# K of the second attention in rows of 8192 B, two tiles a load, with another table of rankings

## The chip, the cores and the metric

The kernel runs on one core of a Trainium2 chip. The metric is the device time of one execution in microseconds; the runs below give it as a median. TensorE (PE) multiplies matrices into PSUM, VectorE (DVE) and ScalarE (ACT) work on SBUF and PSUM, SyncE (SP) issues nearly all transfers from HBM, GpSimd (POOL) sets up constants and issues seven of the output transfers. 16 DMA engines move the data.

## What is computed

Two independent attention blocks, A and B, with cached K and V, and their outputs side by side. A shares one K/V head among eight query heads; B has a K/V head for each of its 32 query heads.

```python
# both: B=16, Sq=32, D=1024, 32 query heads, Sk=1024, Dh=128; all bf16
# A: k_cache, v_cache are (16, 4, 1024, 128); B: (16, 32, 1024, 128)
def _B_ref(x, k_cache, v_cache, wq, wo):
    q = (x @ wq).reshape(B, Sq, H, Dh).transpose(0, 2, 1, 3)
    scores = jnp.einsum("bhqd,bhkd->bhqk", q, k_cache) * (Dh ** -0.5)
    p = _softmax(scores, axis=-1)
    o = jnp.einsum("bhqk,bhkd->bhqd", p, v_cache)
    return o.transpose(0, 2, 1, 3).reshape(B, Sq, H * Dh) @ wo
# A is the same with K and V repeated eight times over the heads
return jnp.concatenate([a, b], axis=-1)
```

K and V of B are 134.2 MB each, K and V of A 16.8 MB each, the four weights 8.4 MB each.

## The kernel before

**Steps.** The work is a list of operations (`pr.add`), built in 128 steps. A step handles one quad of A (four heads of one batch entry, 128 query rows); every second step handles a pair of B: two quads, that is four heads for two batch entries. A pair of B uses four tiles of K and four of V, numbered x = 4 n to 4 n + 3 for pair n. A tile is 512 KB: two heads of one batch entry, 128 partitions by 4096 B.

**K of B.** `tile_src` (L901 to L904) lays two neighbouring heads over the 128 partitions, 16 rows of K (4096 B) on each partition. `st_dmaKB` (L906 to L913) issues the load of one tile on SP. Its place comes from `home_k`: one of eight slots of `KB_sb`, or, for some of the last tiles, a quarter of `wq_sb`, which is no longer needed then. `st_ktrB` (L976) transposes each tile in place on VectorE in blocks of 32 by 32, taking two bf16 as one f32. After this a partition holds a pair of head dimensions, and the free dimension runs over the 16 rows held by a partition and, within these, over 32 source partitions. `st_scoresB` then computes the scores in four passes (`fp`), each a matmul of 512 K columns for each of four tiles x, two quads and two partition groups; the operands are 32 by 32, and 16 matmuls can run beside one another on the sixteen small tiles of the array. L1027 is the line of these matmuls. The bf16 columns are picked with a step of 2, as two head dimensions are interleaved:

```python
rhs = tile_k(4 * q.pn + x)[r0:r0 + 32, :].rearrange("p (s x) -> p s x", s=16)[:, :, o0:o0 + 63:2]
```

**After the scores.** `st_max` (L1038, VectorE) reduces a quad's scores to the negative maximum, `st_exp` (L1051, ScalarE) exponentiates from PSUM into `P2_sb`, and its access pattern puts the columns into the order in which V lies. TensorE then transposes the probabilities (L1097; L1063 is the same for A), they are copied out of PSUM (L651), and L1116 multiplies them with V. L1174 and L1175 normalise; L1190 and L1182 transpose the result for the output projection (L823), whose sums are kept in `acc` (L835, L844). The query projections are L735 (A) and L754 (B); L995 is the score matmul of A, L1083 its product with V, L969 the transposition of its K, L671 that of x at the start.

**Buffers.** There are eight slots for K of B (two pairs), six for V (one and a half), two each for K and V of A. A load is issued on SP when the last reader of the slot's former content has finished; SP takes its instructions in order, so a load that waits holds up those behind it. L891, L898, L910 and L955 are the issues for K of A, V of A, K of B and V of B, L714 those of the query weights, L795 and L805 those of the output weights.

**Order.** `list_schedule` simulates the engines and the transfers with durations written in tables (`DUR` for instructions, `PACKET` for the time of one DMA row by its size) and picks, at each turn, one ready operation by rank. `RANKS` holds 16 ways of ranking, and `TUNE` names for each window of 77 operations which of them applies. The result is the fixed order of each engine, with PSUM banks and work buffers assigned; semaphores are then set for what crosses engines.

Of the kernel before, what the change touches and what calls it, by code (L numbers as in the profile page):

```python
# [43 lines left out]
RANKS = ((3.5, 122, 0.35, 0.0, 0.3), (3.0, 122, 0.35, 0.0, 0.3), (4.0, 122, 0.35, 0.0, 0.3), (3.5, 122, 0.15, 0.0, 0.3), (2.5, 122, 0.35, 0.0, 0.3), (5.0, 122, 0.35, 0.0, 0.3),  # L44
         (3.5, 122, 0.7, 0.0, 0.3), (3.5, 120, 0.35, 0.0, 0.3), (3.0, 124, 0.2, 0.0, 0.3), (3.5, 122, 0.15, 1.5, 0.3), (3.5, 122, 0.15, -1.5, 0.3), (3.5, 122, 0.15, 0.0, 0.0),
         (3.5, 122, 0.15, 0.0, 0.7), (3.5, 122, 0.15, 4.0, 0.3), (3.5, 122, 0.15, -4.0, 0.3), (3.5, 122, 0.25, 0.0, 0.3))
TUNE = (6, 7, 1, 5, 6, 8, 8, 8, 8, 8, 8, 11, 5, 15, 1, 9, 0, 1, 5, 1, 7, 14,
        15, 12, 12, 10, 12, 12, 15, 3, 12, 14, 7, 13, 13, 13, 13, 13, 7, 6, 10, 1, 12, 10,
        3, 12, 0, 11, 9, 12, 7, 13, 12, 11, 12, 3, 4, 10, 14, 9, 9, 10, 4, 0, 0)
HOLD_AHEAD = 1  # L50
STEP_NEAR = 0
TAIL_BASE = 12.0
# [17 lines left out]
    "c0": (0.2, 0.1), "c1": (0.3, 0.1),  # L70
}

PACKET = {"kb_dma": (4096, 0.1592), "vb_dma": (4096, 0.1592), "outh_dma": (1024, 0.049), "wqh_dma": (1024, 0.049)}
PACKET_DEFAULT = (2048, 0.0847)
DMA_ISSUE = 0.45
DMA_FIRST = 1.4
# [3 lines left out]
def dma_time(op):  # L80
    size, us = PACKET.get(op.name, PACKET_DEFAULT)
    return op.dur / size * us / 16
# [45 lines left out]
class Prog:  # L128
# [120 lines left out]
    def list_schedule(self, lat=0.05, look=LOOK):  # L249
# [170 lines left out]
        while True:  # L420
            best = None
            bkey = None
            turn = len(order) // WINDOW
            turn = TUNE[turn] if turn < len(TUNE) else 0
            bl, look, act_first = ranks[turn], RANKS[turn][2], RANKS[turn][4]
# [127 lines left out]
def build(nc, pa, pb, out):  # L553
# [6 lines left out]
    Dh = pa["k"].shape[3]  # L560
    Sk = pa["k"].shape[2]
# [6 lines left out]
    MS = 4  # L568
# [9 lines left out]
    NIT = NSB * NG * 8  # L578
# [7 lines left out]
    pr = Prog()  # L586
    stack = contextlib.ExitStack()
    with stack:
        def sb(name, shape, dt):
            return stack.enter_context(nc.sbuf_tensor(name, shape, dt))  # L590
# [8 lines left out]
        wq_sb = sb("wq_sb", [P, DJ, 2 * CW], BF)  # L599
# [9 lines left out]
        KB_sb = sb("KB_sb", [P, NKB, 16 * Dh], BF)  # L609
# [14 lines left out]
        def bank(v):  # L624
            return psum[:, v.idx, :]
# [7 lines left out]
        for idt, key in ((ident, "ident"), (id32, "id32")):  # L633
            pr.add("pool", lambda g, idt=idt: g.memset(idt[:], 0.0), writes=[key], name="c0")
            pr.add("pool", lambda g, idt=idt: g.affine_select(idt[:], idt[:], [[1, P]], ALU.not_equal, 1.0, base=0, channel_multiplier=-1),
                   writes=[key], name="c1")
# [233 lines left out]
        def mk_quadB(t):  # L870
            q = Quad()
            q.pi = 1
            q.t = t
            q.m = t // (NG * 4)
            q.G = (t // 4) % NG
            jb = t % 4
            q.bp = jb // 2
            q.e = jb % 2
            q.pn = t // 2
            q.b0 = 4 * q.G + 2 * q.bp  # L880
            q.first_of_group = (jb == 0)
            q.last_of_group = (jb == 3)
            q.qid = ("B", t)
            q.kid = ("B", t)
            return q
# [15 lines left out]
        def tile_src(key, x):  # L901
            q, i = quadsB[2 * (x // 4)], x % 4
            h = q.m * MS + 2 * (i % 2)
            return pb[key][q.b0 + i // 2, h:h + 2].rearrange("e (p s) d -> (e p) (s d)", s=16)  # L904

        def st_dmaKB(x):  # L906
            if x < 2 * NIT:
                kind, sl = home_k(x)
                pr.step, was = 2 * ((x - NKB) // 4) if x >= NKB else pr.step, pr.step
                pr.add("sp", lambda e: e.dma_start(tile_k(x), tile_src("k", x)), writes=[(kind, sl)], dma_key=f"{kind.lower()}{sl}", name="kb_dma",  # L910
                       dur=2 * Sk * Dh * 2, wtag={(kind, sl): x})
                pr.step = was

        V_LAST = 2 * NIT - 4
# [12 lines left out]
        def kb_of(x):  # L927
            r = (x - XK) % (NKB + 4)
            assert r >= 4
            return (XK + r - 4) % NKB  # L930

        def home_k(x):
            if x < XK:
                return ("KB", x % NKB)
            return ("wq", (x - XK) % (NKB + 4)) if (x - XK) % (NKB + 4) < 4 else ("KB", kb_of(x))

        def tile_k(x):
            kind, sl = home_k(x)
            return wq_sb[:, 2 * sl:2 * sl + 2, :].rearrange("p j c -> p (j c)") if kind == "wq" else KB_sb[:, sl, :]
# [39 lines left out]
        def both(vS):  # L979
            return psum[:, vS[0].idx:vS[0].idx + 2, :]  # L980

        def score_buf(q):
            q.vS = [Virt("bank", "S"), Virt("bank", "S")]
            q.vst, q.vbo = Virt("stat"), Virt("bank")
# [15 lines left out]
        def p2_of(v):  # L1000
            return P2_sb[:, v.idx, :] if isinstance(v, Virt) else xT_sb[:, v[1], :, :].rearrange("p j t -> p (j t)")[:, 0:2 * Sk]
# [7 lines left out]
        def st_scoresB(qs):  # L1009
            n = qs[0].pn  # L1010
            vP, vPT = (("xT", 0, 0), (("xT", 0, 1), ("xT", 0, 2))) if n >= XT_FREE and n % 2 else (Virt("P2"), (Virt("PT2"), Virt("PT2")))
            for q in qs:
                score_buf(q)
                q.vP, q.vPT, q.vO = vP, vPT, Virt("O2")
            q0 = qs[0]
            gp = (q0.m * NG + q0.G) % 2

            def e_s(e, fp):
                last = None
                o0 = (fp // 2) * 64 + fp % 2  # L1020
                for x in range(4):
                    for q in qs:
                        for g2 in range(2):
                            r0 = 32 * (2 * q.e + g2)
                            lhsT = QR[r0:r0 + 32, gp, 2 * q.bp + x // 2, x % 2, o0:o0 + 63:2]
                            rhs = tile_k(4 * q.pn + x)[r0:r0 + 32, :].rearrange("p (s x) -> p s x", s=16)[:, :, o0:o0 + 63:2]
                            last = e.matmul(bank(q.vS[g2])[32 * x:32 * x + 32, :].rearrange("p (s j) -> p s j", s=16), lhsT, rhs,  # L1027
                                            start=(fp == 0), stop=(fp == 3), tile_position=(r0, 32 * x))
                return last
            qr = [("QR", gp, 2 * q0.bp + t_) for t_ in range(2)]  # L1030
            kt = [(home_k(4 * q0.pn + x), ("T", 4 * q0.pn + x)) for x in range(4)]
            for fp_ in range(4):
                pr.add("pe", lambda e, fp_=fp_: e_s(e, fp_), reads=qr + [r_ for r_, _ in kt], writes=[r_ for q in qs for r_ in q.vS],
                       name="scoresB", tag="B%d" % q0.t, rtag=dict([(r_, (q0.m, q0.G)) for r_ in qr] + kt))
# [6 lines left out]
        def st_exp(q):  # L1041
            vS, vP, vst = q.vS, q.vP, q.vst

            def emit(e):
                if q.pi == 0:
                    src = both(vS).rearrange("p u (c k) -> p k u c", c=NCH // 2)
                    dst = P_sb[:, vP.idx, :].rearrange("p (k u c) -> p k u c", u=2, c=NCH // 2)
                else:
                    src = both(vS).rearrange("p g (s j) -> p g j s", s=16)
                    dst = p2_of(vP)[:, q.e * Sk:(q.e + 1) * Sk].rearrange("p (g j s) -> p g j s", g=2, s=16)  # L1050
                return e.activation(dst, src, ACTF.Exp, bias=stat[:, vst.idx, 0:1], scale=1.0, accum_out=stat[:, vst.idx, 1:2])  # L1051
            pr.add("act", emit, writes=vS + [vP, vst], name="exp")

# [146 lines left out]
        quadsB = [mk_quadB(t) for t in range(NIT)]  # L1200
# [8 lines left out]
        def pairB(n):  # L1209
            qs = [quadsB[2 * n], quadsB[2 * n + 1]]  # L1210
            for x in range(4):
                st_ktrB(4 * n + x)
            if n == 0:
                for x in range(4, NKB):
                    st_dmaKB(x)
            st_scoresB(qs)
            while k_next[0] < min(2 * NIT, 4 * n + 4 + NKB + (4 if n >= LATE else 0)):
                st_dmaKB(k_next[0])
                k_next[0] += 1
            if 4 * n == V_LAST - 8:  # L1220
                for x in (0, 2, 1, 3):
                    st_dmaVB(V_LAST + x)
            for q in qs:
                st_max(q)
                st_exp(q)
            st_ptB(qs)
            if 4 * n == V_LAST:
                st_last(qs)
                return
            st_pvB(qs)  # L1230
            while v_next[0] < min(V_LAST, 4 * n + 4 + NVB + (4 if n >= LATE else 0)):
                st_dmaVB(v_next[0])
                v_next[0] += 1
            for q in qs:
                st_recip(q)
                st_norm(q)
                st_otr(q)
# [30 lines left out]
        for x in range(4):  # L1268
            st_dmaKB(x)
# [90 lines left out]
        if SCHED:  # L1360
            pr = pr.list_schedule()
# [10 lines left out]
def bass_concat_heads__gqa_block_cached__mha_block_cached__near_ridge_kernel(nc, A_x, A_k_cache, A_v_cache, A_wq, A_wo, B_x, B_k_cache, B_v_cache, B_wq, B_wo, out):  # L1372
    build(nc, dict(x=A_x, k=A_k_cache, v=A_v_cache, wq=A_wq, wo=A_wo),
          dict(x=B_x, k=B_k_cache, v=B_v_cache, wq=B_wq, wo=B_wo), out)
# [28 lines left out]
```

## Time and profile before

| | |
|---|---|
| median of three runs | 850.98 us (850.81 to 852.41) |
| span of the profiled execution | 849.5 us |
| PE, DVE, ACT busy | 783.0, 727.0, 623.6 us |
| moved | 341.68 MB, mean 402 GB/s |

The profile is of one execution, and its span runs from its first to its last instruction; the runs' time is taken from outside, so it holds about 1.5 us more. "Busy" of PE counts stretches in which any matmul is under way, and ends of matmuls are modelled. A group's line gives busy time, the mean of one instruction in ns, and the idle time just before its instructions with what ended it. PEld is the weight load, which overlaps the matmuls. SPq is SP's DMA queue. Rates in GB/s are those of all 16 DMA engines.

### The profile page before, as it was taken

What the parts mean: (1) busy time and instruction counts of PE and PEld (TensorE: products, weight loads), DVE (VectorE), ACT (ScalarE), POOL (GpSimd) and SP (SyncE); (2) the same over time, 40 slices, a digit from 0 to 9 for tenths busy, and PEclk for the clock granted to TensorE, in tenths of its full rate; (3) what the DMA queues carried; (4) which work ended last, traced back from release to release, by engine and by line L of the source; (5) the groups of instructions that cost most, each with busy time, mean ns of one, the idle gap of its engine ahead of it and who ended that gap; (6) DMA issues with size and microseconds to landing.
All of it is one profiled execution on the core that took longest, in us unless ns stands there. A gap on an engine that the chain in (4) does not pass through costs nothing.

```text
span 849.5 us, 29749 instructions
## 1 busy us (share of the span) xinstructions
PE 783.0 (92%) x13056; PEld 522.6 (62%) x13056; DVE 727.0 (86%) x1018; ACT 623.6 (73%) x1363; POOL 6.1 (1%) x20
## 2 busy tenths in 40 slices
PE   7989999999898999998999988999899998899878
PEld 4456665666565566665666665666666666666655
DVE  1499987979799898987999898998999978998995
ACT  3497787778677777786788787677877867686874
POOL 1000000000000000000000000000000000000000
PEclk9999999999999999999999999999999999999999
DMA  9999999999999999999999999999999999999995
GB/s 339 415 412 414 411 411 410 405 393 394 416 384 412 409 395 415 416 398 412 414 392 408 411 392 416 415 416 405 410 402 415 412 414 415 415 400 414 416 418 226
DMA packets 112208, 341.68 MB, mean 402 GB/s; under 512 B 12048, under 2 KB 12304, under 8 KB 112080
## 3 DMA queue, kind: packets, MB, share of 16 engines
q1 hardware_dynamic: 111520, 337.95, 100.0%
q8 instruction: 103, 1.69, 0.7%
q0 software_dynamic: 560, 1.84, 0.5%
q14 instruction: 25, 0.20, 0.1%
HBM read 337.64 MB, written 2.10 MB: 400 GB/s over the span
## 4 chain that ended last, share of the span: by engine, by line
PE 55%; DVE 23%; ACT 14%; DMA 5%; issue 2%; SPq 1%; DVEq 0%; ACTq 0%
DVE stat L1038 10%; PE psum L1116 10%; PE psum L823 10%; DVE KB_sb L976 8%; ACT P_sb L1051 8%; PE psum L1027 6%; PE psum L1063 5%; PE psum L754 5%; PE psum L1097 5%; PE psum L1083 4%; DMA KB_sb<-in_B_k_cache_dram 4%; PE psum L995 4%; PE psum L735 4%; ACT PT_sb L651 2%; ACT O_sb L1174 1%
## 5 line engine op out<-in xcount | busy, mean ns | idle before, releaser
L1038 DVE TENSOR_REDUCE stat<-psum 128x1 f32<-128x1024 f32 x256 | 303.6, 1210 | 50.7 <-PE psum L995 31.5
L1051 ACT ACTIVATE P_sb<-psum,stat 128x1024 bf16<-128x1024 f32 x246 | 275.9, 1122 | 63.2 <-DVE stat L1038 59.7
L976 DVE STREAM_TRANSPOSE KB_sb<-KB_sb 128x1024 f32<-128x1024 f32 x240 | 286.6, 1222 | 6.2 <-DMA KB_sb<-in_B_k_cache_dram 6.0
L651 ACT COPY PT_sb<-psum 128x512 f32<-128x512 f32 x226 | 131.4, 604 | 35.2 <-PE psum L1063 22.0
L1116 PE MATMUL psum<-VB_sb,PT_sb 64*64 64x256 bf16 x3584 | 116.2, 271 | 8.6 <-ACT P_sb L1051 5.2
L1116 PEld LDWEIGHTS psum<-VB_sb,PT_sb 64*64 64x64 bf16 x3584 | 97.0, 107 | 27.7 <-issue 25.5
L1174 ACT ACTIVATE O_sb<-psum,stat 128x128 bf16<-128x128 f32 (+1 forms) x205 | 80.8, 417 | 43.2 <-PE psum L1083 23.1
L1063 PE MATMUL psum<-id,P_sb 128*128 128x128 f32 x512 | 88.7, 297 | 6.9 <-ACT P_sb L1051 4.1
L1063 PEld LDWEIGHTS psum<-id,P_sb 128*128 128x128 f32 x512 | 74.0, 208 | 25.2 <-ACT P_sb L1051 13.8
L995 PE MATMUL psum<-KTA_sb,QT_sb 128*128 128x512 bf16 x256 | 84.4, 384 | 3.1 <-ACT P_sb L1051 1.6
L1083 PE MATMUL psum<-VA_sb,PT_sb 128*128 128x128 bf16 x1024 | 78.8, 221 | 7.5 <-ACT P_sb L1051 2.6
L1083 PEld LDWEIGHTS psum<-VA_sb,PT_sb 128*128 128x128 bf16 x1024 | 63.2, 99 | 31.6 <-issue 12.0
L1027 PE MATMUL psum<-KB_sb,QR 32*32 32x512 bf16 x3840 | 73.3, 394 | 8.1 <-ACT P_sb L1051 4.6
L1097 PE MATMUL psum<-id,P_sb 128*128 128x128 f32 x472 | 76.2, 287 | 4.1 <-ACT P_sb L1051 3.5
L754 PE MATMUL psum<-wq_sb,xT_sb 128*128 128x512 bf16 x256 | 72.4, 394 | 3.3 <-DMA wq_sb<-in_B_wq_dram 1.6
L1097 PEld LDWEIGHTS psum<-id,P_sb 128*128 128x128 f32 x472 | 63.8, 193 | 17.3 <-ACT P_sb L1051 7.5
L823 PE MATMUL psum<-woB_sb,OTB_sb 128*128 128x512 bf16 x256 | 66.9, 380 | 2.4 <-ACT P_sb L1051 1.7
L1027 PEld LDWEIGHTS psum<-KB_sb,QR 32*32 32x32 bf16 x3840 | 43.8, 89 | 35.3 <-ACT P_sb L1051 8.3
L823 PE MATMUL psum<-woA_sb,OTA_sb 128*128 128x512 bf16 x256 | 62.8, 380 | 0.4 <-ACT OTA_sb L651 0.3
L735 PE MATMUL psum<-xT_sb,wq_sb 128*128 128x512 bf16 x192 | 54.2, 380 | 1.7 <-issue 1.2
L1051 ACT ACTIVATION_READ_ACCUMULATOR P_sb<-psum,stat 128x1 f32 x246 | 50.3, 205 | 0.0
L835 DVE TENSOR_TENSOR acc<-acc,psum 128x512 f32<-128x512 f32 x64 | 41.3, 675 | 9.6 <-PE psum L823 9.4
(74 smaller groups left out, 720.2 us busy)
## 6 DMA issues: line engine op xcount, KB each, us to landing
KB_sb<-in_B_k_cache_dram SPq DMA_DIRECT2D x240, 512.0 KB, 8.9
VB_sb<-in_B_v_cache_dram SPq DMA_DIRECT2D x234, 512.0 KB, 7.8
KA_sb<-in_A_k_cache_dram SPq DMA_DIRECT2D x64, 256.0 KB, 7.8
VA_sb<-in_A_v_cache_dram SPq DMA_DIRECT2D x64, 256.0 KB, 8.0
wq_sb<-in_B_wq_dram SPq DMA_DIRECT2D x16, 512.0 KB, 8.3
woB_sb<-in_B_wo_dram SPq DMA_DIRECT2D x32, 256.0 KB, 8.5
woA_sb<-in_A_wo_dram SPq DMA_DIRECT2D x32, 256.0 KB, 7.0
wq_sb<-in_B_k_cache_dram SPq DMA_DIRECT2D x16, 512.0 KB, 11.5
```

The lines of the kernel that those rows point to most:

```text
L651: return e.copy(dst, src) if hasattr(e, "activation") else e.tensor_copy(dst, src)
L754: last = e.matmul(bank(v)[:, 0:CW], xT_sb[:, 1, j, G * P:(G + 1) * P], wq_sb[:, j, mh * CW:(mh + 1) * CW], start=(j == 0), stop=(j == DJ - 1))
L823: last = e.matmul(bank(v)[:, 0:OUTW], OT[:, gp, hh, :], wo_[:, hh, oh * OUTW:(oh + 1) * OUTW], start=(hh == 0), stop=(hh == nh - 1))
L976: pr.add("dve", lambda e: e.transpose(tile_k(x).bitcast(F32), tile_k(x).bitcast(F32)), writes=[home_k(x)], name="KBt_tr", rtag={home_k(x): ...
L995: pr.add("pe", lambda e, u=u: e.matmul(bank(vS[u]), qt[:, q.b, q.hh0:q.hh0 + 4, :].rearrange("p a q -> p (a q)"), KTA_sb[:, sl, u * 512:(u ...
L1027: last = e.matmul(bank(q.vS[g2])[32 * x:32 * x + 32, :].rearrange("p (s j) -> p s j", s=16), lhsT, rhs, start=(fp == 0), stop=(fp == 3), t ...
L1038: pr.add("dve", lambda e: e.tensor_reduce(stat[:, vst.idx, 0:1], both(vS), AXIS.XY, ALU.max, negate=True), writes=vS + [vst], name="max")
L1051: return e.activation(dst, src, ACTF.Exp, bias=stat[:, vst.idx, 0:1], scale=1.0, accum_out=stat[:, vst.idx, 1:2])
L1063: last = e.transpose(bank(vb)[:, m * P:(m + 1) * P], p32[:, m:Sk // 2:NPK], id32[:])
L1083: last = e.matmul(bank(vb)[:, 0:Dh], ptc_of(vPT, c, 0, P), VA_sb[:, kvs, c, :], start=(c == 0), stop=(c == NCH - 1))
L1097: last = e.transpose(bank(vb)[:, m * P:(m + 1) * P], p32[:, 4 * h + m:Sk:8], id32[:])
L1116: last = e.matmul(bank(q.vbo)[n0:n0 + 64, 0:2 * Dh].rearrange("p (i d) -> p i d", i=2), pt2_chunk(vPT, c, e0, n0), v2[e0:e0 + 64, :, c, :] ...
```

## The change

- **Loads.** `st_dmaKB` acts for even x alone and loads two tiles, x and x + 1, with one DMA of 1 MB into two neighbouring slots (`tile_k2`). It covers four neighbouring heads of one batch entry. A partition gets 32 rows of K, 8192 B that are contiguous in HBM, and even and odd partitions belong to the first and the second pair of heads.
- **Scores.** After the same transposes in place, one partition's row holds the columns of both head pairs alternating. The score matmul of tile x takes them with a step of 4 bf16 from a start that depends on x % 2: 32 runs of 16 columns, where it was 16 runs of 32.
- **Exponentials.** As a partition holds 32 rows, the order of the columns in PSUM is another, and `st_exp` reads with s = 32 in place of 16 to bring it back to the order of V.
- **Planner.** `PACKET` has 8192 B and 0.3137 us for these loads, and `TUNE` is another table. V's loads, the number of slots, `RANKS` and `DUR` stay.

```diff
-TUNE = (6, 7, 1, 5, 6, 8, 8, 8, 8, 8, 8, 11, 5, 15, 1, 9, 0, 1, 5, 1, 7, 14,
...
+TUNE = (12, 11, 14, 6, 3, 8, 8, 14, 11, 9, 4, 5, 10, 0, 3, 6, 15, 3, 11, 0, 12, 6,
...
-PACKET = {"kb_dma": (4096, 0.1592), "vb_dma": (4096, 0.1592), "outh_dma": (1024, 0.049), "wqh_dma": (1024, 0.049)}
+PACKET = {"kb_dma": (8192, 0.3137), "vb_dma": (4096, 0.1592), "outh_dma": (1024, 0.049), "wqh_dma": (1024, 0.049)}
...
         def st_dmaKB(x):
-            if x < 2 * NIT:
+            if x < 2 * NIT and x % 2 == 0:
                 kind, sl = home_k(x)
                 pr.step, was = 2 * ((x - NKB) // 4) if x >= NKB else pr.step, pr.step
-                pr.add("sp", lambda e: e.dma_start(tile_k(x), tile_src("k", x)), writes=[(kind, sl)], dma_key=f"{kind.lower()}{sl}", name="kb_dma",
-                       dur=2 * Sk * Dh * 2, wtag={(kind, sl): x})
+                q = quadsB[2 * (x // 4)]
+                src = pb["k"][q.b0 + x % 4 // 2, q.m * MS:q.m * MS + MS].rearrange("(i e) (r s) d -> (e r) i (s d)", e=2, s=32)
+                pr.add("sp", lambda e: e.dma_start(tile_k2(x), src), writes=[(kind, sl), (kind, sl + 1)], dma_key=f"{kind.lower()}{sl}", name="kb_dma",
+                       dur=4 * Sk * Dh * 2, wtag={(kind, sl): x, (kind, sl + 1): x + 1})
                 pr.step = was
...
+        def tile_k2(x):
+            kind, sl = home_k(x)
+            assert x % 2 == 0 and sl % 2 == 0 and home_k(x + 1) == (kind, sl + 1)
+            return (wq_sb[:, 2 * sl:2 * sl + 4, :] if kind == "wq" else KB_sb[:, sl:sl + 2, :]).rearrange("p j c -> p (j c)")
...
-                            rhs = tile_k(4 * q.pn + x)[r0:r0 + 32, :].rearrange("p (s x) -> p s x", s=16)[:, :, o0:o0 + 63:2]
-                            last = e.matmul(bank(q.vS[g2])[32 * x:32 * x + 32, :].rearrange("p (s j) -> p s j", s=16), lhsT, rhs,
+                            k2 = tile_k2(4 * q.pn + x // 2 * 2)[r0:r0 + 32, :].rearrange("p (s x) -> p s x", s=32)
+                            rhs = k2[:, :, o0 + 2 * (x % 2):(fp // 2) * 64 + 64:4]
+                            last = e.matmul(bank(q.vS[g2])[32 * x:32 * x + 32, :].rearrange("p (s j) -> p s j", s=32), lhsT, rhs,
                                             start=(fp == 0), stop=(fp == 3), tile_position=(r0, 32 * x))
...
-                    src = both(vS).rearrange("p g (s j) -> p g j s", s=16)
-                    dst = p2_of(vP)[:, q.e * Sk:(q.e + 1) * Sk].rearrange("p (g j s) -> p g j s", g=2, s=16)
+                    src = both(vS).rearrange("p g (s j) -> p g j s", s=32)
+                    dst = p2_of(vP)[:, q.e * Sk:(q.e + 1) * Sk].rearrange("p (g j s) -> p g j s", g=2, s=32)
```

More of the change, by code (lines that the diff above doesn't have):

```diff
@@ L46 @@
          (3.5, 122, 0.15, 0.0, 0.7), (3.5, 122, 0.15, 4.0, 0.3), (3.5, 122, 0.15, -4.0, 0.3), (3.5, 122, 0.25, 0.0, 0.3))
-TUNE = (6, 7, 1, 5, 6, 8, 8, 8, 8, 8, 8, 11, 5, 15, 1, 9, 0, 1, 5, 1, 7, 14,
-        15, 12, 12, 10, 12, 12, 15, 3, 12, 14, 7, 13, 13, 13, 13, 13, 7, 6, 10, 1, 12, 10,
-        3, 12, 0, 11, 9, 12, 7, 13, 12, 11, 12, 3, 4, 10, 14, 9, 9, 10, 4, 0, 0)
+TUNE = (12, 11, 14, 6, 3, 8, 8, 14, 11, 9, 4, 5, 10, 0, 3, 6, 15, 3, 11, 0, 12, 6,
+        13, 10, 5, 4, 0, 4, 11, 0, 3, 11, 10, 7, 12, 9, 11, 9, 3, 3, 0, 15, 8, 10,
+        9, 11, 2, 12, 9, 13, 15, 8, 1, 4, 9, 12, 11, 12, 8, 9, 8, 4, 13, 0, 0)
 HOLD_AHEAD = 1
```

## The prediction

> **What bounds the kernel now.** I read the totals first, then three stretches, then the waits, then the chain of waits. The totals of the page:
>
> ```profile
> span 849.5 us, 29749 instructions
> PE 783.0 (92%) x13056; PEld 522.6 (62%) x13056; DVE 727.0 (86%) x1018; ACT 623.6 (73%) x1363; POOL 6.1 (1%) x20
> q1 hardware_dynamic: 111520, 337.95, 100.0%
> ```
>
> The transfers of SP's queue keep the 16 DMA engines occupied for the whole span, and TensorE is busy for 92% of it. Two resources are near full, so the stretches decide (columns: stretch, its length, busy of PE, PEld, DVE, ACT and POOL with counts, granted clock, DMA share, GB/s):
>
> ```profile
> 0.00:25.00 25.00, 18.65 (x119) 10.32 (x120) 4.08 (x6) 8.36 (x10) 2.19 (x13) 1.00 0.95 351
> 25.00:825.00 800.00, 745.01 (x12506) 499.97 (x12520) 708.31 (x985) 603.85 (x1326) 2.84 (x5) 1.00 1.03 408
> 825.00:850.00 25.00, 19.37 (x449) 12.26 (x424) 14.66 (x29) 11.45 (x29) 1.08 (x2) 0.97 0.62 248
> ```
>
> Over the 800 us between start and end the transfers run at 408 GB/s and PE idles 55 us in sum. What 408 is to be held against, a quiet stretch from 325 to 350 us shows: the rates in 40 slices of 0.625 us, and what was issued there.
>
> ```profile
> GB/s 419 419 426 400 406 413 426 419 419 419 419 419 419 410 423 383 410 413 416 419 416 420 419 416 423 400 406 420 419 420 419 420 419 420 419 426 410 420 423 433
> KB_sb<-in_B_k_cache_dram SPq DMA_DIRECT2D x9, 512.0 KB, 9.3
> VB_sb<-in_B_v_cache_dram SPq DMA_DIRECT2D x8, 512.0 KB, 9.4
> KA_sb<-in_A_k_cache_dram SPq DMA_DIRECT2D x2, 256.0 KB, 8.1
> VA_sb<-in_A_v_cache_dram SPq DMA_DIRECT2D x2, 256.0 KB, 9.0
> ```
>
> K and V of the second attention come in 128 rows of 4096 B a load, those of the first in rows of 2048 B. The plateau of 419 to 420 I read as 4096 B rows; the short dips to 400 to 406, about two slices long each, as the 2048 B loads, since one K and V pair of 512 KB takes two slices. So a 4096 B row costs 4096 B x 16 / 420 GB/s = 156.0 ns of an engine, and a 2048 B row at 403 GB/s 81.3 ns.
>
> ```profile
> HBM read 337.64 MB, written 2.10 MB: 400 GB/s over the span
> ```
>
> Of these 337.6 MB, 268.4 (K and V of the second attention, 134.2 each by the reference's shapes) are in 4096 B rows and most of the rest in 2048 B rows: a full queue would run the mix at about 416 GB/s. Against 408 that leaves 800 us x (1 - 408/416) = 15 us in which the queue was thin. So the middle is within 2% of what the DMA engines can do with these rows.
>
> The waits say the other half:
>
> ```profile
> DVE KB_sb L976 <- DMA KB_sb<-in_B_k_cache_dram: 6.0, 6, 3.1
> ACT P_sb L1051 <- DVE stat L1038: 59.7, 71, 4.1
> DVE stat L1038 <- PE psum L995: 31.5, 25, 8.5
> SPq L955 <- PE psum L1116: 109.9, 36, 6.9
> SPq L910 <- PE psum L1027: 57.0, 24, 5.1
> ```
>
> VectorE waits for a K tile 6 times, 6.0 us in all. SP waits for TensorE to release buffers far longer. So the loads run into the backpressure of the buffers: the transfers are saturated, yet the work hardly ever stands still for them. The chain that ended last agrees:
>
> ```profile
> PE 55%; DVE 23%; ACT 14%; DMA 5%; issue 2%; SPq 1%; DVEq 0%; ACTq 0%
> DVE stat L1038 10%; PE psum L1116 10%; PE psum L823 10%; DVE KB_sb L976 8%; ACT P_sb L1051 8%; PE psum L1027 6%; PE psum L1063 5%; PE psum L754 5%; PE psum L1097 5%; PE psum L1083 4%; DMA KB_sb<-in_B_k_cache_dram 4%; PE psum L995 4%; PE psum L735 4%; ACT PT_sb L651 2%; ACT O_sb L1174 1%
> ```
>
> ```profile
> 25.51 12.86 DMA KB_sb<-in_B_k_cache_dram
> 198.67 10.08 DMA KB_sb<-in_B_k_cache_dram
> 303.07 10.12 DMA KB_sb<-in_B_k_cache_dram
> 313.22 4.92 DVE KB_sb L976 x4
> ```
>
> The long DMA pieces in it are three K loads, and after 303 us there is none. The planner has laid the compute out at the pace of the transfers, and the two run side by side with a slack of one buffer. That is what makes this change hard to call: faster transfers alone do not shorten a chain made of compute; the new order must use them.
>
> **The change part by part.** The sum is made against the profiled span of 849.5 us; about 1.5 us lie around it, since the median of the runs is 850.98.
>
> Rows of K. 240 loads into KB_sb and 16 into wq_sb are now 128 loads of 1 MB:
>
> ```profile
> KB_sb<-in_B_k_cache_dram SPq DMA_DIRECT2D x240, 512.0 KB, 8.9
> wq_sb<-in_B_k_cache_dram SPq DMA_DIRECT2D x16, 512.0 KB, 11.5
> ```
>
> 256 x 128 = 32768 rows of 4096 B become 16384 of 8192 B, 1024 for each of 16 engines. The trace has no such row for data. From the two rows that it has, the part that does not grow with size is 2 x 81.3 - 156.0 = 6.6 ns a row, so 8192 B would cost 2 x 156.0 - 6.6 = 305.4 ns (429 GB/s), and each merge saves 6.6 ns: 1024 x 6.6 ns = 6.8 us. The planner's own table in the diff implies 2 x 159.2 - 313.7 = 4.7 ns, or 4.8 us; I take that as its assumption only. Lower end: no saving, if the engine works an 8192 B row as two of 4096 B. A loss has no row for it, as the step from 2048 to 4096 B gained. I take 6 us off the DMA engines' time.
>
> [...]
>
> How much of it reaches the end? All of it if the order follows, none if the chain of compute is rigid. PE has 55 us of idle time in the middle to give, so following is possible, but the chain after 303 us holds no DMA. I take two thirds, 4 us.
>
> Issues and granularity. Four issues in a row take 1.75 us on SP:
>
> ```profile
> 404.02 1.75 SPq L955 DMA_DIRECT2D VB_sb<-in_B_v_cache_dram  x4
> ```
>
> 128 DMA instructions fewer save some 128 x 0.44 us there, but SP holds 1% of the chain: 0, at best 1 us. The first tile of a pair now lands with the second, 512 KB later: 512 KB at 419 GB/s is 1.25 us. What hides it is the prefetch of eight K slots, by which only 6 transposes of 256 waited; without that cover it is 6 x 1.25 = 7.5 us, with the maxima L1038 queued behind the transposes on DVE, and the exponentials L1051 behind those. A V load queued behind K can also be late by 1.25 us, and no wait of PE for VB_sb is listed. The release is unchanged: all four score passes read all four K tiles, so both slots of a load come free at the same instruction. I put 0.
>
> Scores. Each of the 64 matmuls of a pair streams 512 K columns as before, but 8 B apart instead of 4 B, in runs of 16 instead of 32:
>
> ```profile
> 410.33 1.19 PE L1027 MATMUL psum<-KB_sb,QR 32*32 32x512 bf16 x64
> 404.54 0.59 PE L995 MATMUL psum<-KTA_sb,QT_sb 128*128 128x512 bf16 x2
> L1027 PE MATMUL psum<-KB_sb,QR x3840: 371/393/429, 40.7 to 830.8; 32*32 32x512 bf16 x192
> L671 PEld LDWEIGHTS psum<-ident,acc x64: 142/147/171, 3.6 to 17.8; 128*128 128x128 bf16 x64
> L969 PEld LDWEIGHTS psum<-ident,KA_sb x512: 95/98/111, 13.6 to 803.0; 128*128 128x128 bf16 x171
> ```
>
> 16 matmuls run at once on the 16 small tiles: (1.19 - 0.39) / 3 = 0.27 us a wave, against 0.59 - 0.38 = 0.21 us for one dense matmul of 512 columns. So 4 B spacing with four streams on each row group costs at most a little. For wider spacing the nearest row is a weight load: L671 reads bf16 elements 16 B apart and takes 147 ns, the dense L969 98 ns, 49 ns more for 128 elements, or 0.38 ns each. 8 B is a third of the way from 4 to 16: 0.13 ns x 512 x 256 waves = 17 us of PE at one end, 0 at the other; with the full 0.38 ns it is 50 us. I take 0: dense single streams and four 4 B streams both run near a column a cycle, and the weight load is another path.
>
> [...]
>
> The exponentials read PSUM at steps of 64 B instead of 128 B. One group holds those of the first attention, at steps of 512 B, and those of the second:
>
> ```profile
> L1051 ACT ACTIVATE P_sb<-psum,stat x246: 1107/1115/1204, 38.3 to 834.2; 128x1024 bf16<-128x1024 f32 x123
> L976 DVE STREAM_TRANSPOSE KB_sb<-KB_sb x240: 1200/1225/1247, 21.9 to 828.7; 128x1024 f32<-128x1024 f32 x120
> ```
>
> 1107 to 1204 ns for both: the step is free. The transposes keep their shape: 0.
>
> The other table of rankings. It adds no instruction; it changes which ready operation goes first, in all 65 windows of the plan. Its bounds are the 15 us of thin queue: a better order wins back part of it, a worse one adds as much. I take 0.
>
> Sum: 849.5 - 4 = 845.5 us of span, about 847 with what lies around it.
>
> **The rivals.**
>
> Hidden anyway: the chain of compute after 303 us is rigid, or an 8192 B row costs as much as two. For it: 6.0 us of waits for K in the whole run. Against it: DMA at 98% of its rate, and an order drawn up anew for the new cost. Time: 851.
>
> ```profile
> L1027 PE MATMUL psum<-KB_sb,QR 32*32 32x512 bf16 x3840 | 73.3, 394 | 8.1 <-ACT P_sb L1051 4.6 <-issue 0.9 <-ACT PT_sb L651 0.9
> L1027 PE MATMUL psum<-wq_sb,QR 32*32 32x512 bf16 x256 | 4.8, 395 | 1.1 <-ACT xT_sb L651 0.6 <-DVE stat L1165 0.5
> ```
>
> The scores take longer, the slower one. Place: L1027, at the read of K. Price: 17 us of PE. The two groups of L1027 above are 73.3 + 4.8 = 78 us busy, and 6% of 849.5 us, 51 us, lie on the chain, so two thirds of what is added show, 11 us: 849.5 + 11 + 1.5 = 862, and about 884 with the 50 us. It decides as soon as the chain share of the added time exceeds the 4 us won, that is from 6 us on PE, 24 ns a wave (0.27 to 0.29 us). Against it: 4 B spacing shows no slope.
>
> A worse order: half as much thin queue again, 7.5 us, against the 4 us won: 854.5. For it: the thin stretches come from the order, and the order is new everywhere. Against it: it is as likely to fall the other way.
>
> **How the numbers follow.** Transfers gain and the order follows: 0.55, 842 to 849, forecast 847. Hidden: 0.15, 850 to 852. Scores longer: 0.14, 855 to 884. Worse order: 0.16, 852 to 860. A measurement of this kernel can tell about 0.2%, 1.7 us, from no change, so faster 0.55, same 0.15, slower 0.30. The range is 841 to 861: it leaves out some 0.10 above and 0.06 below.
>
> **What would show it.** Right: packets drop by 16384 and the rate in quiet stretches rises above 420 where K lands; a wave of scores stays near 0.27 us and PE's busy time near 783; L976 waits for K stay near 6 us; the gain lies between 25 and 825 us. Wrong: L1027 dearer (scores rival), quiet stretches at 420 (rows no faster), a mean between 25 and 825 us below 408 GB/s with a full rate in the quiet stretches (order), or a higher rate while PE's idle time grows.

## The result and the profile after

The changed kernel takes 896.11 us (median of 4 runs, 894.02 to 899.46), beside 851.69 us for the kernel before on the same chip: a ratio of 1.0525, 95% interval 1.0497 to 1.0554. It is 5% slower, where 0.5% faster was forecast, and lies far above the stated range of 841 to 861. First the totals, a middle stretch and the chain of the changed kernel (columns as before):

```profile
span 895.3 us, 29488 instructions
PE 819.3 (92%) x12925; PEld 530.3 (59%) x13056; DVE 741.0 (83%) x1039; ACT 617.9 (69%) x1342; POOL 6.1 (1%) x20
q1 hardware_dynamic: 93088, 337.94, 95.5%
...
PE 64%; ACT 15%; DVE 14%; DMA 4%; issue 2%; SPq 1%; DVEq 0%; ACTq 0%
PE psum L1035 14%; PE psum L823 10%; ACT P_sb L1059 9%; DVE stat L1046 9%; PE psum L1124 9%; PE psum L1105 5%; PE psum L1071 5%; PE psum L735 5%; PE psum L1091 4%; PE psum L754 4%; PE psum L1002 4%; DVE KB_sb L983 3%; DMA VB_sb<-in_B_v_cache_dram 2%; PE psum L976 2%; ACT O_sb L1182 1%
```

```profile
25.00:870.00 845.00, 783.05 (x12426) 508.48 (x12565) 724.38 (x1014) 597.72 (x1308) 2.85 (x5) 1.00 0.99 393
```

The score matmuls of B, L1027 before and L1035 now, have gone from 6% of the chain to 14% and are its first entry. PE's own share went from 55 to 64%. The transfers no longer fill the span (95.5%), and the rate between start and end fell from 408 to 393 GB/s. The groups of the score matmuls and their durations (minimum, median, maximum in ns) say how much:

```profile
L1035 PE MATMUL psum<-KB_sb,QR 32*32 32x512 bf16 x3840 | 125.9, 630 | 5.9 <-ACT P_sb L1059 3.3 <-ACT OTB_sb L651 0.7 <-ACT OTA_sb L651 0.5
L1035 PE MATMUL psum<-wq_sb,QR 32*32 32x512 bf16 x256 | 8.3, 628 | 0.9 <-ACT P_sb L1059 0.9
```

```profile
417.16 2.09 PE L1035 MATMUL psum<-KB_sb,QR 32*32 32x512 bf16 x64
```

One matmul takes 630 ns instead of 394, the 64 of a pair 2.09 us instead of 1.19, and the two groups together 134.2 us instead of 78.1: 56 us more of PE. (The page's total for PE grew by only 36 us, but 131 matmul records are missing from this trace: 12925 of 13056 are there, and 202 of the 256 score matmuls of A.) The maxima on VectorE, the exponentials on ScalarE behind them and the transposes of K wait longer than before:

```profile
ACT P_sb L1059 <- DVE stat L1046: 101.3, 89, 7.5
DVE stat L1046 <- PE psum L1035: 51.9, 50, 3.0
...
DVE KB_sb L983 <- DMA KB_sb<-in_B_k_cache_dram: 14.2, 11, 5.3
```

The wait of the maxima for the scores of B has gone from 16.0 us to 51.9 us; the row of the kernel before:

```profile
DVE stat L1038 <- PE psum L1027: 16.0, 25, 2.1
```

With the scores late, buffers come free late, and the transfers run dry; the rates of the changed kernel from 550 to 575 us, in 40 slices of 0.625 us, show it, and the pieces of the chain and the issues beside them (start, length) show where the holes end:

```profile
GB/s 419 459 426 459 419 393 433 419 433 344 403 400 295 108 49 66 92 223 406 433 406 393 433 419 413 406 419 420 426 420 426 420 413 380 144 20 7 210 0 315
556.51 2.00 PE psum L1035 x33
558.63 1.19 SPq L912 DMA_DIRECT2D KB_sb<-in_B_k_cache_dram  x2
570.09 2.00 PE psum L1035 x36
572.21 1.19 SPq L912 DMA_DIRECT2D KB_sb<-in_B_k_cache_dram  x2
```

There are two holes, down to 49 and to 0. In both, the next two K loads (L912) go out at 558.63 and 572.21 us, about 0.1 us after a set of score matmuls ends (558.51 and 572.09). There are also several slices of 433 to 459 GB/s, where the stretch of before had one of 433. A single slice tells little of the rate: one row of 8192 B more or less in 0.625 us is 13 GB/s.

### The profile page after: what moved, and what is told of

It reads as the page before. It is cut to its first block, busy times and chain, and to the rows that moved or that the text cites. A ratio compares the mean times of both kernels' runs of the same rounds, so it can differ in the third digit from the quotient of the medians.

```text
span 895.3 us, 29488 instructions
## 1 busy us (share of the span) xinstructions
PE 819.3 (92%) x12925; PEld 530.3 (59%) x13056; DVE 741.0 (83%) x1039; ACT 617.9 (69%) x1342; POOL 6.1 (1%) x20
## 3 DMA queue, kind: packets, MB, share of 16 engines
q1 hardware_dynamic: 93088, 337.94, 95.5%
## 4 chain that ended last, share of the span: by engine, by line
PE 64%; ACT 15%; DVE 14%; DMA 4%; issue 2%; SPq 1%; DVEq 0%; ACTq 0%
PE psum L1035 14%; PE psum L823 10%; ACT P_sb L1059 9%; DVE stat L1046 9%; PE psum L1124 9%; PE psum L1105 5%; PE psum L1071 5%; PE psum L735 5%; PE psum L1091 4%; PE psum L754 4%; PE psum L1002 4%; DVE KB_sb L983 3%; DMA VB_sb<-in_B_v_cache_dram 2%; PE psum L976 2%; ACT O_sb L1182 1%
## 5 line engine op out<-in xcount | busy, mean ns | idle before, releaser
L1046 DVE TENSOR_REDUCE stat<-psum 128x1 f32<-128x1024 f32 x256 | 305.2, 1215 | 80.1 <-PE psum L1035 51.9
L1059 ACT ACTIVATE P_sb<-psum,stat 128x1024 bf16<-128x1024 f32 x246 | 275.5, 1120 | 104.5 <-DVE stat L1046 101.3
L983 DVE STREAM_TRANSPOSE KB_sb<-KB_sb 128x1024 f32<-128x1024 f32 x240 | 285.6, 1220 | 14.3 <-DMA KB_sb<-in_B_k_cache_dram 14.2
L651 ACT COPY PT_sb<-psum 128x512 f32<-128x512 f32 x217 | 125.4, 601 | 40.2 <-PE psum L1071 21.2
L1035 PE MATMUL psum<-KB_sb,QR 32*32 32x512 bf16 x3840 | 125.9, 630 | 5.9 <-ACT P_sb L1059 3.3
L1182 ACT ACTIVATE O_sb<-psum,stat 128x128 bf16<-128x128 f32 (+1 forms) x197 | 78.8, 418 | 42.7 <-PE psum L1091 27.6
L1035 PEld LDWEIGHTS psum<-KB_sb,QR 32*32 32x32 bf16 x3840 | 50.1, 89 | 52.0 <-issue 21.0
L1002 PE MATMUL psum<-KTA_sb,QT_sb 128*128 128x512 bf16 x202 | 68.8, 380 | 6.8 <-ACT P_sb L1059 2.3
L754 PE MATMUL psum<-wq_sb,xT_sb 128*128 128x512 bf16 x239 | 68.6, 388 | 4.5 <-DMA wq_sb<-in_B_wq_dram 2.2
L823 PE MATMUL psum<-woB_sb,OTB_sb 128*128 128x512 bf16 x234 | 62.4, 379 | 4.6 <-issue 1.6
L735 PE MATMUL psum<-xT_sb,wq_sb 128*128 128x512 bf16 x170 | 48.2, 379 | 2.5 <-issue 1.8
```

The source lines that it names most:

```text
L651: return e.copy(dst, src) if hasattr(e, "activation") else e.tensor_copy(dst, src)
L754: last = e.matmul(bank(v)[:, 0:CW], xT_sb[:, 1, j, G * P:(G + 1) * P], wq_sb[:, j, mh * CW:(mh + 1) * CW], start=(j == 0), stop=(j == DJ - 1))
L823: last = e.matmul(bank(v)[:, 0:OUTW], OT[:, gp, hh, :], wo_[:, hh, oh * OUTW:(oh + 1) * OUTW], start=(hh == 0), stop=(hh == nh - 1))
L983: pr.add("dve", lambda e: e.transpose(tile_k(x).bitcast(F32), tile_k(x).bitcast(F32)), writes=[home_k(x)], name="KBt_tr", rtag={home_k(x): ...
L1002: pr.add("pe", lambda e, u=u: e.matmul(bank(vS[u]), qt[:, q.b, q.hh0:q.hh0 + 4, :].rearrange("p a q -> p (a q)"), KTA_sb[:, sl, u * 512:(u ...
L1046: pr.add("dve", lambda e: e.tensor_reduce(stat[:, vst.idx, 0:1], both(vS), AXIS.XY, ALU.max, negate=True), writes=vS + [vst], name="max")
```

## The experiments

Three things changed at once: the spacing at which the scores read K, the loads, and the order. The theory after the result was that the spacing alone explains it (theory 1); its rivals were the order (2, later O) and the loads (3, later L). Each ratio is against runs of the kernel before on the same chip; single runs of that kernel lie between 848.06 and 855.84 us, so a single run below tells no difference smaller than that.

**The changed kernel, reading at 4 B again.**

```diff
-    rhs = k2[:, :, o0 + 2 * (x % 2):(fp // 2) * 64 + 64:4]
+    rhs = tile_k(4 * q.pn + x)[r0:r0 + 32, :].rearrange("p (s x) -> p s x", s=16)[:, :, o0:o0 + 63:2]
```

> The changed kernel with one edit: the score matmuls read K as before, 4 B apart in runs of 32, from their own half of the loaded pair (so the columns of two heads are mixed and the scores are other numbers; the count and shape of all work stay). Loads of 1 MB, new rankings and order are kept. Theory 1 (the 8 B step halves the rate of the score matmuls, and all of the loss comes from there): a score matmul returns from 628 to about 393 ns, PE busy falls by some 50 us to 765-785, and the time is 843 to 850. Theory 2 (the new order is worse by itself): 393 ns, but the time stays at 870 or more. Theory 3 (a 1 MB load into two slots starves VectorE): 393 ns, waits for K stay at 14 us or more, time 855 to 870.

Measured: 858.79 us beside 850.05, ratio 1.0084 (1.0050 to 1.0119). The totals, the score group and VectorE's wait for K in this kernel:

```profile
PE 786.0 (92%) x13056; PEld 524.8 (61%) x13056; DVE 738.2 (86%) x1039; ACT 618.0 (72%) x1342; POOL 6.1 (1%) x20
...
L1034 PE MATMUL psum<-KB_sb,QR 32*32 32x512 bf16 x3840 | 74.0, 398 | 7.5 <-ACT P_sb L1058 3.3
```

```profile
DVE KB_sb L983 <- DMA KB_sb<-in_B_k_cache_dram: 22.7, 19, 5.2
```

With the spacing undone, 36 of the 44 us are gone, and the matmul is back at 398 ns. The second half of theory 1 fell: what is left of the change is still 0.8% slower, not faster. The time and the waits of 22.7 us are what theory 3 expected for this kernel. The exponentials still wait 86.3 us for the maxima here, against 59.7 before and 101.3 in the changed kernel, so most of that growth does not come from the spacing.

**The kernel before, reading at 8 B.** Each of the four streams reads its own tile.

```diff
-    rhs = tile_k(4 * q.pn + x)[r0:r0 + 32, :].rearrange("p (s x) -> p s x", s=16)[:, :, o0:o0 + 63:2]
+    rhs = tile_k(4 * q.pn + x)[r0:r0 + 32, :].rearrange("p (s x) -> p s x", s=32)[:, :, fp:64:4]
```

> The kernel before with one edit: the score matmuls read their own K tile 8 B apart, in 32 runs of 16 (the same data in another sequence, so the scores are other numbers). 512 KB loads and the old rankings are kept, and no two of the four streams touch the same tile. Theory 1: 393 ns become about 628 ns, PE busy rises by about 50 us, the time is 885 to 905. Theory 2: the matmuls get longer but the time stays under 865. A rival on the cause, that two streams reading the same places of a shared tile get in each other's way: 393 ns and 851 us.

Measured: 892.72 us, ratio 1.0494 (1.0462 to 1.0525).

```profile
PE 830.8 (93%) x13056; PEld 528.3 (59%) x13056; DVE 728.1 (82%) x1018; ACT 624.3 (70%) x1363; POOL 6.1 (1%) x20
...
L1027 PE MATMUL psum<-KB_sb,QR 32*32 32x512 bf16 x3840 | 123.1, 624 | 8.0 <-ACT P_sb L1051 4.3
```

One access pattern, put into the kernel before with nothing else, makes nearly the whole loss: 43 us of time from 48 us more of PE. Two streams in one shared tile are not needed for it. The parts do not simply add up: undoing the spacing wins 36 us, putting it in alone costs 43, and the rest of the change costs 9 by itself, against 44 for all together.

**Run length.** The same spacing as before, in runs of 16:

```diff
+    rhs = tile_k(4 * q.pn + x)[r0:r0 + 32, :].rearrange("p (s x) -> p s x", s=32)[:, :, 32 * (fp // 2) + fp % 2:32 * (fp // 2) + 32:2]
```

> The kernel before with one edit: the score matmuls read their own K tile 4 B apart as before, but in 32 runs of 16 instead of 16 runs of 32 (other numbers as scores). It takes the run length apart from the spacing. Theory 1 (spacing): 393 ns and 851 us. Rival (short runs cost): above 500 ns and above 870 us.

Measured: 852.71 us, ratio 1.0025 (0.9980 to 1.0070).

```profile
L1027 PE MATMUL psum<-KB_sb,QR 32*32 32x512 bf16 x3840 | 74.4, 400 | 9.2 <-ACT P_sb L1051 4.3
```

With 400 ns a matmul, beside 394, short runs are not the cause.

**The law of the spacing.** Three kernels, each the kernel before with the spacing of the score reads alone set to 2, 6 and 16 B:

```diff
+    rhs = tile_k(4 * q.pn + x)[r0:r0 + 32, :].rearrange("p (s x) -> p s x", s=4)[:, fp, :]               # 2 B
+    rhs = tile_k(4 * q.pn + x)[r0:r0 + 32, 128 * fp + fp:128 * fp + fp + 1536:3]                        # 6 B
+    rhs = tile_k(4 * q.pn + x)[r0:r0 + 32, :].rearrange("p (j k) -> p k j", k=8)[:, 2 * fp:2 * fp + 2, :] # 16 B
```

> The kernel before with one edit: each score matmul of B reads 512 neighbouring columns of its own K tile, 2 B apart (the same data in another sequence; the scores are other numbers). It shows whether 4 B already costs something. Laws A and B: 393 ns and 849 to 853 us as before. Rival (cost grows from 2 B on): below 380 ns.

> The kernel before with one edit: each score matmul of B reads 512 columns of its own K tile 6 B apart (some columns are left out, others are read in another pass, so the scores are other numbers). [...] Law A (the time grows with the bytes spanned, free up to 4 B): 1.5 times 213 plus 180 ns, about 500 ns, and 870 to 880 us. Law B (anything above 4 B takes two cycles a column): about 625 ns, and 885 to 897 us.

> The kernel before with one edit: each score matmul of B reads its own K tile 16 B apart, in 2 runs of 256 (the same data in another sequence; the scores are other numbers). Law A: four times 213 plus 180 ns, about 1030 ns, and above 960 us. Law B: two cycles a column whatever the distance, about 625 ns and 885 to 897 us.

Measured, one run each: 852.06, 866.78 and 1005.72 us. The instructions of the score line in the kernels with 2, 6, 8 and 16 B, in this order (minimum, median, maximum in ns):

```profile
L1027 PE MATMUL psum<-KB_sb,QR x3840: 371/374/604, 40.7 to 831.5; 32*32 32x512 bf16 x192
```

```profile
L1027 PE MATMUL psum<-KB_sb,QR x3840: 494/502/532, 40.9 to 846.1; 32*32 32x512 bf16 x192
```

```profile
L1027 PE MATMUL psum<-KB_sb,QR x3840: 602/626/662, 40.6 to 871.5; 32*32 32x512 bf16 x192
```

```profile
L1027 PE MATMUL psum<-KB_sb,QR x3840: 1052/1074/1144, 42.1 to 984.4; 32*32 32x512 bf16 x192
```

With 393 ns at 4 B the medians are 374, 393, 502, 626 and 1074 ns. From 4 to 16 B this is close to a straight line, (1074 - 393) / 12 = 57 ns a byte for 512 columns, with 55, 62 and 56 between neighbours. Law A holds from 4 B on, though the time at 6 B lies 3 us below the range that it gave; law B (about 625 ns above 4 B, whatever the distance) falls. No run shows the 213 ns for 512 columns with which law A's sums were made; from 4 to 16 B they show 227 ns for each 4 B of spacing (681 / 3), which leaves 166 ns of the 393. At 2 B the matmul is 19 ns shorter than at 4 B, some 10 ns a byte. That is below the 380 ns named for the rival, so 4 B is not quite free, but the line is far flatter there; the time of 852.06 us shows no gain.

**One, two or four streams.** The kernel before, with the score matmuls of A (one stream) and the V product of B (two on a group of rows) at 8 B:

```diff
-    KTA_sb[:, sl, u * 512:(u + 1) * 512]
+    KTA_sb[:, sl, :].rearrange("p (j k) -> p k j", k=4)[:, 2 * u:2 * u + 2, :]
...
-    v2[e0:e0 + 64, :, c, :]      # tiles as "p i (s d) -> p i s d", s=16
+    v3[e0:e0 + 64, :, c // 4, :, c % 4]      # tiles as "p i (s d k) -> p i s d k", s=4, k=4
```

> The kernel before with two edits elsewhere: the score matmuls of A (one stream over all 128 partitions) and the product with V in B (two streams on each 64 partitions) read their moving operand 8 B apart instead of densely; the score matmuls of B stay at 4 B. Scores and outputs are other numbers. Theory S (the four streams of a row group share a limited reading, about one 16 B place a cycle): A's score matmul stays near 384 ns and the V product near 271 ns, time 849 to 855. Rival (every stream pays for 8 B by itself): A's score matmul near 590 ns, the V product near 375 ns, time above 900.

Measured, one run: 990.49 us. The groups of the V product and of A's scores, first in the kernel before, then in this one:

```profile
L1116 PE MATMUL psum<-VB_sb,PT_sb 64*64 64x256 bf16 x3584 | 116.2, 271 | 8.6 <-ACT P_sb L1051 5.2 <-issue 2.5 <-ACT KTA_sb L651 0.4
L995 PE MATMUL psum<-KTA_sb,QT_sb 128*128 128x512 bf16 x256 | 84.4, 384 | 3.1 <-ACT P_sb L1051 1.6 <-ACT PT_sb L651 0.3 <-ACT QR L651 0.2
```

```profile
L1116 PE MATMUL psum<-VB_sb,PT_sb 64*64 64x256 bf16 x3584 | 225.3, 404 | 7.2 <-ACT P_sb L1051 4.9 <-issue 1.5 <-DVE acc L835 0.6
L995 PE MATMUL psum<-KTA_sb,QT_sb 128*128 128x512 bf16 x256 | 142.5, 619 | 2.4 <-ACT P_sb L1051 1.4 <-ACT PT_sb L651 0.3 <-ACT acc L651 0.2
```

Theory S, a reading shared by the four streams of a row group, fell. From 2 to 8 B a single stream goes from 384 to 619 ns, by 235 ns, and four side by side went from 374 to 626 above, by 252 ns. The V product, two side by side with half the columns, takes 133 ns more, which would be 266 for 512. So each of the streams measured pays by itself, and by nearly the same amount, whether it has company or not; what makes the differences of up to 13% is not shown.

**A repair.** The transposition on VectorE writes the two head pairs side by side, and the scores read 4 B apart:

```diff
+    e.transpose(tile_k(x).bitcast(F32).rearrange("p (b i r) -> p b r i", i=2, r=16), tile_k(x).bitcast(F32).rearrange("p (b r i) -> p b r i", i=2, r=16))
...
+    o1 = o0 + 32 * (x % 2)
+    rhs = k2[:, :, o1:o1 + 31:2]
```

> The changed kernel, repaired: the transposition on VectorE writes the columns of the two head pairs side by side within each block of 32 instead of alternating, so the score matmuls read 4 B apart again, in runs of 16. Loads of 1 MB and the new order are kept. Theory 1: score matmuls near 393 ns; if the transposition keeps its 1.22 us, the time is 843 to 850, faster than before. If its scattered writes cost more, each 0.1 us adds 26 us to VectorE's busy time, and from some 0.3 us a transposition the time is above 890 again.

Measured: 975.09 us, ratio 1.1453 (1.1417 to 1.1488). Score matmuls 408 ns, but the transposition:

```profile
DVE 69%; PE 23%; ACT 5%; issue 1%; DMA 1%; SPq 0%; DVEq 0%; ACTq 0%
...
L983 DVE STREAM_TRANSPOSE KB_sb<-KB_sb 128x1024 f32<-128x1024 f32 x240 | 446.3, 1922 | 5.3 <-DMA KB_sb<-in_B_k_cache_dram 5.3
```

A transposition takes 1922 instead of 1222 ns. In this group alone VectorE is busy 160 us longer (446.3 against 286.6 us), more than the 122 us that it had idle before (849.5 - 727.0), and it holds 69% of the chain. The cost was moved to another engine and is larger there than the 56 us of the scores.

**What is left: loads or order.** Two kernels cross them at 4 B spacing. In the first, the order is that of before, and only the K loads are joined, as one of 1 MB in rows of 8192 B at the place of the first:

```diff
+    if name == "kb_dma":                  # where the finished order is written out
+        if emit.tile % 2 == 1:
+            continue
+        writes = (writes[0], (writes[0][0], writes[0][1] + 1))
...
+    src = pb["k"][b, h:h + 4].rearrange("(i e) (r s) d -> (e r) i (s d)", e=2, s=32)
```

> The kernel before with its own order of every engine, but each two K loads are one of 1 MB in rows of 8192 B, at the place of the first of the two; the score matmuls read 4 B apart in runs of 32 as before (columns of two heads are mixed, so the scores are other numbers). Against the 858.8 us of the changed kernel at 4 B spacing this splits the 8 us that are left into loads and order. Theory O (the new order costs them): 844 to 850 us, as the rows gain. Theory L (1 MB loads come too late for VectorE): 854 to 862 us, with waits of VectorE for K well above the 6 us of before.

In the second, the order is the new one, and each K load is issued as two of 512 KB in rows of 4096 B:

```diff
+    emit.halves = [(lambda e, y=y: e.dma_start(tile_k(y), tile_src("k", y)), home_k(y)) for y in (x, x + 1)]
...
+    for half, home in emit.halves:        # where the finished order is written out
+        newp.add(eng, half, actual(reads), (home,), f"{home[0].lower()}{home[1]}", name, dur, tag, prio)
```

> The changed kernel at 4 B spacing in its own new order, but each K load is issued as two of 512 KB in rows of 4096 B, as before the change, one behind the other. (Score columns then lie as in the kernel before, with the exponentials reordered for the other layout, so the result is other numbers.) Theory O: 856 to 866 us, no better than 858.8, as the order keeps its cost and the rows lose their gain. Theory L: 848 to 853 us.

A third takes the 1 MB loads in the order of before, but with rows of 4096 B, two on a partition:

```diff
-    src = pb["k"][b, h:h + 4].rearrange("(i e) (r s) d -> (e r) i (s d)", e=2, s=32)
+    src = pb["k"][b, h:h + 4].rearrange("(i e) (p s) d -> (e p) i (s d)", e=2, s=16)
```

> The kernel before with its own order, two K loads joined to one DMA of 1 MB at the place of the first, but in rows of 4096 B, two rows on each partition; layout, scores and result as before. Beside the kernel with 1 MB in rows of 8192 B (ratio 1.0048) it tells granularity from row size. If granularity costs and the longer rows gain part of it back: a ratio of 1.006 to 1.012. If granularity costs and rows gain nothing: 1.003 to 1.006. If the row size itself costs: 1.000 +- 0.002.

| order | K loads | ratio (95% interval) | share of SP's transfers x span | waits of VectorE for K |
|---|---|---|---|---|
| before | 512 KB, 4096 B | 1 | 849.5 us | 6.0 us |
| before | 1 MB, 4096 B | 1.0046 (1.0027 to 1.0065) | 845.4 us | 12.9 us |
| before | 1 MB, 8192 B | 1.0048 (1.0024 to 1.0072) | 840.4 us | 13.5 us |
| new | 512 KB, 4096 B | 1.0057 (1.0039 to 1.0075) | 847.6 us | 7.2 us |
| new | 1 MB, 8192 B | 1.0084 (1.0050 to 1.0119) | 840.6 us | 22.7 us |

The ratios are of all runs; the last two columns are each of one profiled execution, and the fourth is the share in the queue's line times the span. The rows behind the second and third lines, first 4096 B, then 8192 B, and behind the fourth:

```profile
q1 hardware_dynamic: 109472, 337.94, 99.8%
...
L988 DVE STREAM_TRANSPOSE KB_sb<-KB_sb 128x1024 f32<-128x1024 f32 x240 | 286.3, 1221 | 13.2 <-DMA KB_sb<-in_B_k_cache_dram 12.9
```

```profile
q1 hardware_dynamic: 93088, 337.94, 98.9%
...
L988 DVE STREAM_TRANSPOSE KB_sb<-KB_sb 128x1024 f32<-128x1024 f32 x240 | 286.3, 1222 | 13.9 <-DMA KB_sb<-in_B_k_cache_dram 13.5
```

```profile
PE 784.0 (92%) x13056; PEld 524.5 (61%) x13056; DVE 738.1 (86%) x1039; ACT 617.2 (72%) x1342; POOL 6.1 (1%) x20
q1 hardware_dynamic: 111520, 337.95, 99.3%
...
DVE KB_sb L989 <- DMA KB_sb<-in_B_k_cache_dram: 7.2, 4, 4.1
```

Neither O nor L alone: joined loads cost about 0.5% in the old order, with either row size, and the new order costs about 0.6% with the old loads (855.34 us, which lies between the ranges of both theories). The longer rows seem to take time off the DMA engines, 5.0 us against 1 MB loads of 4096 B in the old order and 7.0 us against the 512 KB loads in the new one. These sizes are rough, as the three lines with rows of 4096 B differ by up to 4.1 us among themselves. The time does not follow: between the second and the third line it stays the same within 0.3%.

What makes the two half per cents was not found. The waits for K do not show it: the executions profiled in the second and third lines were the fastest of their kernels (848.93 us, median 853.61; 851.61 us, median 856.60), and their spans of 847.1 and 849.8 us are within 0.3% of the 849.5 us of before, although the waits for K had more than doubled. The new order differs in more than the sequence: the planner also chooses the engine of some copies, and 21 instructions and 11 us of work have moved to VectorE (x1039 and 738.1 us, against x1018 and 727.0). The granted clock of TensorE is lower there as well, 0.990 on average against 0.996 in the runs of the kernel before beside it. Whether one of these costs the time is open.

**The table alone.** The kernel before with the new `TUNE`, and so a plan of its own:

```diff
-TUNE = (6, 7, 1, 5, 6, 8, 8, 8, 8, 8, 8, 11, 5, 15, 1, 9, 0, 1, 5, 1, 7, 14,
...
+TUNE = (12, 11, 14, 6, 3, 8, 8, 14, 11, 9, 4, 5, 10, 0, 3, 6, 15, 3, 11, 0, 12, 6,
...
```

> The kernel before with the other table of rankings alone: loads, rows, spacing and planner costs as before. The plan is drawn up anew, so the order is neither that of before nor that of the changed kernel. Theory O in its stronger form (a table fits one set of costs, and another table costs some us): 854 to 866 us. Rival (tables are interchangeable): 848 to 853 us.

Measured: 877.71 us, ratio 1.0305 (1.0271 to 1.0338). The middle of this kernel:

```profile
25.00:855.00 830.00, 762.94 (x12561) 501.56 (x12558) 729.75 (x1026) 594.38 (x1296) 3.37 (x6) 0.98 1.01 397
```

The rate falls from 408 to 397 GB/s, with no instruction added. The loss is larger than theory O's range of 854 to 866 us. Under the old costs the table loses 27 us; under its own costs (new order, old loads) the loss was 5 us. That fits a table that suits only the costs it was drawn up for, but no wait or chain was followed to show how the 27 us arise. The granted clock is 0.981 to 0.988 in these runs. None of the kernels run is faster than the one before.

## Why the prediction was wrong, by its steps

**The scores: the step that failed.** Put at 0, from two rows: 0.21 us for the 512 columns of a dense single stream and 0.27 us for a wave of four streams at 4 B, with the weight load at 16 B set aside as another path. No trace shows how long a cycle is; what the two rows show is 0.41 and 0.52 ns a column. In place of the 0 the runs show 56 us of PE, and 48 us from the 8 B spacing alone in the kernel before. The two rows used could not carry the 0: both lie at or below the bend at 4 B, and the one row beyond it, the weight load at 16 B, did show a slope. The upper end of 50 us, from 0.38 ns a column, was near the truth, though not by its reasoning, and the rival's place was right, with a price of 17 us that came from drawing a line between 4 and 16 B on a weight load's terms (its dense row, L969, reads 2 B apart). A moving operand has a steeper line: 0.11 ns a column and byte (57 ns / 512), so 8 B costs 0.46 ns a column. The share that reaches the end was too low as well: two thirds was taken, and the kernel before with 8 B lost 43 us of 48 us. The rival's range of 855 to 884 us ends below the 896.11 us measured for this reason, and because the order and the loads cost something beside it.

**The rows.** The sum's 6 us on the DMA engines was about right, as far as single executions tell: 5.0 and 7.0 us in the two orders. That two thirds of it, 4 us, reach the end was wrong: no gain was seen (1.0048 beside 1.0046, and in the new order 1.0084 beside 1.0057). The rival "hidden anyway" had this term right, and the sign that spoke for it, 6.0 us of waits for K in the whole run, weighed more than the full queue.

**Granularity.** Put at 0, with 7.5 us as the price without cover. Joined loads cost 0.5%, some 4 us, so the 0 was too low. The waits for K rose from 6.0 to 13.5 us, by just the 7.5 us, but that agreement is luck: there were 14 waits, not 6 longer ones, and the execution that shows them was no slower than the kernel before.

**The order.** Put at 0, within 15 us either way. The new order costs 0.6% at equal loads, about 5 us, which is inside the bound. But the reason for the bound, the thin queue of before, does not hold in general: the table alone, under the old costs, loses 27 us. The step also took the table to change the sequence alone, while it moves work from ScalarE to VectorE as well.

**Right.** The exponentials (1120 ns) and the transposes of the changed kernel (1220 ns) kept their durations, and SP holds 1% of the chain as before, so its saved issues showed nowhere.

## What to carry to other kernels

Before a layout is changed to please the transfers, write down the spacing at which every reader will then meet the data: here a saving of 5 to 7 us on the DMA engines, which never reached the end, was bought with score matmuls of 630 instead of 394 ns. If no row of the profile lies on the far side of the new spacing, a probe of one access pattern in the old kernel is cheap and answers it alone. The queue was 100% occupied here, yet VectorE waited for K for only 6.0 of 849.5 us, and longer rows did not shorten the time (ratio 1.0048 beside 1.0046): that a resource is full does not by itself make it the bound.

## What the runs showed of the hardware

The time of a bf16 score matmul of 512 columns hardly grows from 2 to 4 B between the columns of its moving operand (374 and 393 ns). From there it grows with the spacing (502, 626 and 1074 ns at 6, 8 and 16 B), about 57 ns a byte, which is 9 B of span a nanosecond and partition (512 B / 57 ns). From 2 to 8 B the cost is nearly the same for one stream over 128 partitions (235 ns) and for sixteen small ones at once (252 ns), and runs of 16 or 32 columns make no difference at 4 B (400 and 394 ns). A block transposition on VectorE that writes its columns in another sequence within the block takes 1922 instead of 1222 ns.
